# A transform that begins with one product alone: single raw blocks, later low parts on VectorE, last rows normalised on ScalarE

## The chip, the cores and the metric

The kernel runs on one core of one Trainium2 chip. The metric is the device time of one execution in microseconds (us). The kernel before takes 1825.14 us (median of three runs, 1822.15 to 1827.36).

## The reference

Four layers follow one another: a Fourier layer, an attention layer, the same Fourier layer, the same attention layer. Each adds its result to its input and takes the layer-normalised input. There are 2048 rows of 512 float32 numbers.

```python
def _A_ref(x, dft_seq_re, dft_seq_im, dft_hid_re, dft_hid_im):
    a = jnp.einsum("bsd,ed->bse", x, dft_hid_re)
    b = jnp.einsum("bsd,ed->bse", x, dft_hid_im)
    return jnp.einsum("ts,bse->bte", dft_seq_re, a) - jnp.einsum("ts,bse->bte", dft_seq_im, b)

x = A_x
x = x + _A_ref(_layernorm(x), A_dft_seq_re, A_dft_seq_im, A_dft_hid_re, A_dft_hid_im)
x = x + _B_ref(_layernorm(x), B_wq, B_wk, B_wv, B_wo, B_beta)
x = x + _A_ref(_layernorm(x), A_dft_seq_re, A_dft_seq_im, A_dft_hid_re, A_dft_hid_im)
x = x + _B_ref(_layernorm(x), B_wq, B_wk, B_wv, B_wo, B_beta)
```

`_B_ref` is attention with 32 heads over four segments of 512 rows, with a memory that is carried from segment to segment. The change lies in the second Fourier layer, called transform two here.

## The kernel before

**Products.** The kernel multiplies with the sequence matrices first and with the hidden matrices after that. The sequence part uses a Strassen-like scheme: seven products, P1 to P7 in the code's names, for each of four column groups (`tcn` 0 to 3) of 512 output rows. Every product sums over eight row blocks (`k` 0 to 7). A product at one `k` takes a left operand from the normalised rows (`xa[i]`, 16 tiles of 128 rows; `xb` and `xs` for P6, P5 and P3) and a right operand from the sequence matrix. Both are split into a high and a low part: `split` (L90 to 102) makes the high part by an ACT copy that rounds, and the low part by a subtraction, on DVE unless told otherwise. `matmul3` then does three matmuls (high-high, high-low, low-high) for each of two column halves. So one `k` of one product is six matmuls of 128x512. This document calls it a step, and the code's clock for transform two counts in steps.

**Right operands.** Blocks of the sequence matrix (256 KB each, `ct`) and sums that transform one left in memory (`sums`) are loaded into raw buffers. `read_pair` (L418) loads two blocks for a pair of products, adds or subtracts them on DVE (L426), and splits both blocks; `one_right` gives the split operand a tile of tag `chi` and one of tag `clo` by turns, three buffers of each. The attention layer before uses the same buffers for its stacks. `read_two` (L434) loads two `k` of one product.

**Raw buffers.** `raw_pair` (L316) hands out pairs of blocks. There are four pairs in the tile `cring`, and two more in `craw` once the attention before no longer uses it. The pair that was released longest ago is taken.

**Left operands.** `normalise` (L204) loads two rows tiles, normalises them on DVE (L166), lets POOL subtract one half from the other for rows 0 to 7 (L225), and splits: high part on ACT, low part on POOL (the groups with `xa` at L98). The last four tiles also need their moments: `bn_stats` on DVE, a power on POOL (L145) and four small DVE operations. `add_rows` (L252) loads tiles `k` and `k + 8` again, normalises both on DVE, combines them by three half-width DVE operations (L260 to 262) and splits the results into `xb[k]` and `xs`.

**Order.** Each part is a Python generator that `place` puts at steps. At a step, generators run in the order of their first argument, and the program is emitted in that order. A planner then sets the order within each engine. Matmuls, the high parts on ACT (`pin`) and the additions of L426 keep their emitted order; other instructions may move. Each engine executes its own queue in order; loads go through SP's queue. Before the change, steps 0 to 63 hold P1 and P7 by turns for groups 0 to 3 and steps 64 to 127 hold P2 and P4 by turns. P6, P5 and P3 follow from step 128. The two rows tiles of `normalise` are placed at steps -40, -24, -8, 2, 24, 34, 46 and 54. `add_rows(k)` is placed at 84 + 6k. The last units of the attention before overlap the first 36 steps or so.

Of the kernel before, what the change touches and what calls it, by code (L numbers as in the profile page):

```python
# [10 lines left out]
F32 = mybir.dt.float32  # L11
# [7 lines left out]
P = 128  # L19
# [37 lines left out]
def spectral_infini_kernel(  # L57
# [136 lines left out]
    joined = [dram.tile([P, 4, 256], F32, name=f"join{k}") for k in range(HALF)]  # L194
    row_mv = consts.tile([P, NT, 2], F32, name="row_mv")
    row_r = consts.tile([P, NT], F32, name="row_r")

    def measure(s, i, xr):
        moments(row_mv[:, s * LT + i], xr)
# [4 lines left out]
    def place_spectral(x_in, x_out, t0, end, ln_at, direct):  # L204
# [4 lines left out]
        def normalise(n):  # L209
            leads = n[0] == 0 and direct  # L210
            xt = [load_rows(x_in[i]) for i in n]
            yield
            some = slice(n[0], n[-1] + 1, max(1, n[-1] - n[0]))
            known = not direct and n[-1] < NT - LT
            if not known:
                with behind_first(direct and not leads):
                    ve, r = row_stats(xt, row_mv[:, some])
            yield
            if not known:
                row_scale(row_r[:, some], ve, r)  # L220
            for i, src in zip(n, xt):
                with nullcontext() if direct else behind_max():
                    xn = normal(src, row_mv[:, i], row_r[:, i : i + 1])
                if not direct and i < HALF:
                    G.tensor_tensor(  # L225
                        out=xn[:, D // 2 :], in0=xn[:, : D // 2], in1=xn[:, D // 2 :], op=ALU.subtract
                    )
                xa[i] = pair("xa", "w", 16)
                engines = {"lo_engine": V if direct else G, "hi_engine": V if leads else A}
                lo = split(xa[i][:, 0], xa[i][:, 1], xn, **engines)  # L230
                plain[i] = xn
                if leads:
                    first_row.append(lo[1])
            yield
            if not direct or n[-1] < HALF:
                return
            k = n[-1] - HALF
            e, o = plain[k], plain[k + HALF]
            a, b = slice(0, D // 2), slice(D // 2, D)
            low = sb.tile([P, 512], F32, name="low", tag="praw", bufs=2)  # L240
            top = sb.tile([P, 3, 256], F32, name="top", tag="parts", bufs=2)
            with behind_first(n[0] == HALF):
                pin(V.tensor_tensor(out=low[:, a], in0=e[:, a], in1=e[:, b], op=ALU.subtract))
                pin(V.tensor_tensor(out=top[:, 1], in0=o[:, b], in1=e[:, b], op=ALU.subtract))
                pin(V.tensor_tensor(out=top[:, 0], in0=e[:, a], in1=top[:, 1], op=ALU.add))
                pin(V.tensor_tensor(out=top[:, 2], in0=top[:, 0], in1=o[:, a], op=ALU.subtract))
            yield
            nc.sync.dma_start(joined[k][:, 0], low[:, a])
            nc.sync.dma_start(joined[k][:, 1:], top)
            yield  # L250

        def add_rows(k):  # L252
            xt = [load_rows(x_in[i]) for i in (k, k + HALF)]
            yield
            e, o = (
                normal(xt[n], row_mv[:, i], row_r[:, i : i + 1])
                for n, i in enumerate((k, k + HALF))
            )
            a, b = slice(0, D // 2), slice(D // 2, D)
            V.tensor_tensor(out=e[:, b], in0=o[:, b], in1=e[:, b], op=ALU.subtract)  # L260
            V.scalar_tensor_tensor(e[:, a], e[:, a], -1.0, e[:, b], op0=ALU.mult, op1=ALU.subtract)
            V.scalar_tensor_tensor(o[:, a], e[:, a], -1.0, o[:, a], op0=ALU.mult, op1=ALU.subtract)
            xb[k] = pair("xb", "w", 16)
            split(xb[k][:, 0], xb[k][:, 1], e)
            if k % 2 == 0:
                xs[k // 2] = pair("xs", "w", 16)
            half = xs[k // 2][:, :, k % 2 * 256 : (k % 2 + 1) * 256]
            split(half[:, 0], half[:, 1], o[:, a])
            yield
# [43 lines left out]
            }[name]  # L313
            return src[:, h, (col + m) * P : (col + m + 1) * P]

        def raw_pair(own=False):  # L316
            clock[0] += 1
            if not homes:
                ring = sb.tile([P, 2 * LT, 512], F32, name="cring", tag="xT", bufs=1)
                homes.extend(ring[:, j : j + 2] for j in range(0, 2 * LT, 2))  # L320
                if direct:
                    homes.extend(pair("craw", "craw", 2, F32) for _ in range(2))
                    homes.extend(spare[:, j : j + 2] for j in range(0, 6, 2))
            elif not direct and len(homes) == LT and clock[0] > 24:
                homes.extend(pair("craw", "craw", 2, F32) for _ in range(2))
            j = min((j for j in range(LT if own else len(homes)) if released.get(j, 0) is not None), key=lambda j: released.get(j, 0))
            released[j] = None
            return homes[j], j

# [87 lines left out]
            release(*(j for _, j in held))  # L417
            yield  # L418

        def read_pair(tcn, k, names):  # L420
            two, j = raw_pair()
            fetch(two[:, 0], ct[tcn, k, :, BLOCK[names[0]]])
            fetch(two[:, 1], summed(tcn, k, "P6"))
            yield
            op = ALU.subtract if names[1] == "P7" else ALU.add
            pin(V.tensor_tensor(out=two[:, 1], in0=two[:, 1], in1=two[:, 0], op=op))  # L426
            yield
            right[tcn, names[0], k] = one_right(two[:, 0])
            yield
            right[tcn, names[1], k] = one_right(two[:, 1])  # L430
            release(j)
            yield

        def read_two(tcn, k, name):  # L434
            two, j = raw_pair(tcn == TC - 1 and name != "P6")
            for h in range(2):
                fetch(two[:, h], ct[tcn, k + h, :, BLOCK[name]] if name in BLOCK else summed(tcn, k + h, name))
            yield
            right[tcn, name, k] = one_right(two[:, 0])
            yield  # L440
            right[tcn, name, k + 1] = one_right(two[:, 1])
            release(j)
            yield

# [137 lines left out]
        if direct:  # L582
            place(2, contract(0), run_from(t, 4 * HALF, 2))
            for k in range(HALF):
                place(3, read_plain(0, k), [t + 8 * k + d for d in (-12, -4, 1, 4)])
                place(3, change_rows(k), [t + 8 * k + d for d in (5, 9)])
            t += 8 * HALF
            names = "P1", "P2", "P7", "P4"
            for tcn in range(1, TC):
                for n, name in enumerate(names):  # L590
                    place(2, product(tcn, name), run_from(t + n, HALF, 4))
                for k in range(HALF):
                    place(3, read_all(tcn, k), [t + 4 * k + d for d in (-11, -6, -4, -2, -1)])
                t += 4 * HALF
            for k in range(HALF):
                place(3, join_rows(k), [t + 5 * k + d for d in (-33, -27)])
            for tcn in range(1, TC):
                for n, name in enumerate(CHAIN):
                    place(2, product(tcn, name), run_from(t + n, HALF, 3))
                for k in range(0, HALF, 2):  # L600
                    place(3, read_rest(tcn, k), [t + 3 * k + d for d in (-12, -6, -3, 0)])
                t += 3 * HALF
        else:
            for names in ("P1", "P7"), ("P2", "P4"):
                for tcn in range(TC):
                    for n, name in enumerate(names):
                        place(2, product(tcn, name), run_from(t + n, HALF, 2))
                    for k in range(HALF):
                        place(3, read_pair(tcn, k, names), [t + 2 * k + d for d in (-10, -6, -4, -3)])
                    t += 2 * HALF  # L610
            for k in range(HALF):
                place(3, add_rows(k), [t - 48 + 6 * k, t - 44 + 6 * k])
            for tcns in (0, 1), (2, 3):
                at = {tcn: [] for tcn in tcns}
                for name, tcn in itertools.product(CHAIN, tcns):
                    at[tcn] += run_from(t, HALF)
                    for k in range(0, HALF, 2):
                        place(3, read_two(tcn, k, name), [t + k + d for d in (-9, -4, -3)])
                    t += HALF
                for tcn in tcns:  # L620
                    place(2, chained(tcn), at[tcn])
# [679 lines left out]
```

## Time and profile before

| what | value |
|---|---|
| median of three runs | 1825.14 us (1822.15 to 1827.36) |
| the profiled execution | 1827.82 us, span 1825.6 us |
| PE (TensorE matmul) busy | 1752.3 us, 96% of the span |
| DVE (VectorE) busy | 1417.2 us, 78% |
| ACT (ScalarE) busy | 1095.1 us, 60% |
| POOL (GpSimd) busy | 493.7 us, 27% |
| first and last matmul of transform two's sequence products | 901.1 us and 1245.6 us |

PE is TensorE's matmul stream, PEld its weight loads, SP the engine whose queue issues most transfers. Times in a timeline or a table of stretches are microseconds from the start of the span. An idle time in square brackets is the engine's idle time just before the instruction, with what ended it. Durations of neighbouring instructions of one engine overlap a little, so the distance of two starts is the price of one in a run of instructions.

### The profile page before, as it was taken

How to read it: one execution, taken by the hardware profiler on the slowest of the kernel's cores; microseconds unless marked ns; L12 is line 12 of the kernel's file. 1: busy time of each engine (PE TensorE's matmuls, PEld its weight loads, DVE VectorE, ACT ScalarE, POOL GpSimd, SP SyncE). 2: the span in 40 equal slices, each digit the busy share in tenths (PEclk: the TensorE clock that was granted, in tenths of full speed). 3: DMA queues.
4: the chain of work that ended last, by engine and by line, in shares of the span. 5: the costliest groups of instructions: out<-in, count | busy, mean ns of one | idle time of the engine just before them, and what ended most of it. 6: DMA issues, size and time to landing. Idle time of an engine off the chain costs nothing.

```text
span 1825.6 us, 32144 instructions
## 1 busy us (share of the span) xinstructions
PE 1752.3 (96%) x10192; PEld 1263.1 (69%) x10192; DVE 1417.2 (78%) x4240; ACT 1095.1 (60%) x2359; POOL 493.7 (27%) x805
## 2 busy tenths in 40 slices
PE   8999999999999999999899999999998999999998
PEld 6888777877556665665568787888875666666655
DVE  8888977764877978878877898667658778787785
ACT  3344443432987877777764444444428887877785
POOL 1000000013443444354531000000134443544442
PEclk9999999999999999999999999999999999999999
DMA  8777765355443534433565666544545434344341
GB/s 285 252 265 234 248 218 176 115 179 163 157 134 97 165 115 132 140 124 117 170 193 197 204 226 230 196 162 133 169 144 175 134 119 156 114 134 142 107 127 44
DMA packets 168345, 300.70 MB, mean 165 GB/s; under 512 B 19440, under 2 KB 70640, under 8 KB 168176
## 3 DMA queue, kind: packets, MB, share of 16 engines
q1 hardware_dynamic: 158000, 285.29, 48.3%
q10 hardware_dynamic: 10176, 13.37, 2.0%
q8 instruction: 80, 1.31, 0.3%
q14 instruction: 89, 0.73, 0.1%
HBM read 209.73 MB, written 88.08 MB: 163 GB/s over the span
## 4 chain that ended last, share of the span: by engine, by line
PE 68%; DVE 12%; DMA 4%; issue 3%; ACT 2%; POOL 1%; SPq 0%; DVEq 0%; ACTq 0%; POOLq 0%
PE m L82 17%; PE pqk L82 9%; PE y L82 8%; PE pv_bank L82 7%; PE sT L82 7%; PE nat L82 6%; PE pvv L82 4%; PE po L82 4%; DVE junk L791 3%; DMA stkk<-scrk 1%; DVE c L499 1%; DVE clo L98 1%; PE pm L82 1%; PE on L82 1%; PE pM L82 1%
## 5 line engine op out<-in xcount | busy, mean ns | idle before, releaser
L791 DVE CUSTOM_DVE_ANT_0 junk<-nat,mask 128x512 bf16<-128x512 f32 (+3 forms) x1024 | 496.7, 485 | 159.6 <-PE nat L82 124.4
L860 ACT ACTIVATE pT<-sT 128x512 f32<-128x512 f32 x640 | 371.8, 599 | 14.9 <-DVE sT L857 1.4
L863 POOL TENSOR_SCALAR_AFFINE_SELECT pT<-pT 128x256 f32<-128x256 f32 (+1 forms) x448 | 203.2, 467 | 474.1 <-ACT pT L860 376.9
L82 PE MATMUL m<-chi,xa 128*128 128x512 f32 x1056 | 310.3, 394 | 3.7 <-DVE c L499 2.1
L82 PE MATMUL nat<-stkk,stkq 96*128 96x512 bf16 (+3 forms) x1024 | 246.3, 302 | 10.2 <-DVE mx L791 6.7
L82 PE MATMUL sT<-stkq,stkk 99*128 99x256 bf16 (+3 forms) x1024 | 250.2, 306 | 4.4 <-ACT pT L860 1.8
L82 PE MATMUL m<-clo,xa 128*128 128x512 f32 x720 | 235.1, 398 | 7.4 <-DVE clo L98 7.4
L859 ACT ACTIVATE sT<-sT 128x256 f32<-128x256 f32 (+1 forms) x628 | 205.0, 336 | 51.8 <-PE sT L82 49.3
L82 PEld LDWEIGHTS m<-chi,xa 128*128 128x128 f32 x1056 | 199.2, 189 | 47.1 <-DVE c L499 2.9
L82 PE MATMUL y<-wdt,us 128*128 128x512 f32 x768 | 182.3, 391 | 0.2 <-DVE wdt L98 0.2
L82 PEld LDWEIGHTS <-stkk 99*128 99x128 bf16 x1024 | 81.9, 98 | 132.8 <-issue 120.5
L82 PEld LDWEIGHTS m<-clo,xa 128*128 128x128 f32 x720 | 135.7, 190 | 42.0 <-DVE clo L98 14.5
L82 PEld LDWEIGHTS y<-wdt,us 128*128 128x128 f32 x768 | 143.5, 188 | 30.4 <-DVE wdt L98 0.9
L82 PE MATMUL pv_bank<-pT,v_all 128*17 128x512 f32 (+3 forms) x2048 | 154.7, 440 | 1.1 <-POOL pT L863 1.1
L96 ACT ACTIVATE chi<-cring 128x512 fp32r<-128x512 f32 (+1 forms) x137 | 99.1, 727 | 90.4 <-PE m L82 41.3
L145 POOL TENSOR_TENSOR r<-ve,half_neg 128x2 f32<-128x2 f32 (+2 forms) x24 | 19.9, 828 | 451.5 <-DVE ve L143 448.7
L82 PEld LDWEIGHTS <-stkq 96*128 96x128 bf16 x1024 | 94.6, 99 | 64.5 <-issue 21.8
L82 PE MATMUL pvv<-wv,xT 128*128 128x512 f32 x384 | 127.3, 443 | 3.6 <-DVE mx L791 3.6
L82 PE MATMUL pqk<-xT,wq 128*128 128x512 f32 x384 | 129.9, 448 | 0.0
L82 PE MATMUL po<-wo,oh 128*128 128x512 f32 x384 | 123.6, 438 | 3.1 <-DVE mx L791 2.2
L82 PE MATMUL pqk<-xT,wk 128*128 128x512 f32 x384 | 123.4, 430 | 0.0
L82 PEld LDWEIGHTS pv_bank<-pT,v_all 128*17 128x17 f32 x2048 | 53.5, 98 | 90.2 <-issue 85.1
(187 smaller groups left out, 3003.6 us busy)
## 6 DMA issues: line engine op xcount, KB each, us to landing
cring<-sum SPq DMA_DIRECT2D x105, 256.0 KB
stkq<-scrq SPq DMA_DIRECT2D x64, 384.0 KB
stkk<-scrk SPq DMA_DIRECT2D x64, 384.0 KB
cring<-in_ct SPq DMA_DIRECT2D x80, 256.0 KB
xt<-mid SPq DMA_DIRECT2D x64, 256.0 KB
cring<-in_ct SPq DMA_DIRECT2D x27, 512.0 KB
mid<-xr SPq DMA_DIRECT2D x48, 256.0 KB
scrq<-parts SPq DMA_DIRECT2D x32, 384.0 KB
```

Of the source, the lines that this page charges most:

```text
L82: return tc.keep_in_program_order(op(*args, **kwargs))
L96: pin(A.activation(hi, src, AF.Copy, scale=scale))
L98: lo_engine.tensor_tensor(out=lo, in0=src, in1=hi.bitcast(F32), op=ALU.subtract)
L145: G.tensor_tensor(out=r, in0=ve, in1=half_neg[:, :n], op=ALU.pow)
L499: V.tensor_tensor(out=dst, in0=c[tcn, base][:, m], in1=ps[m], op=op)
L791: last_max[0] = V.tensor_tensor_reduce(junk[:, :n], src, mask[:, 512 - n :], 1.0, 3e38, ALU.add, ALU.min, dst,)
L859: A.activation(blocks, blocks, AF.Relu)
L860: A.activation(dst, ps, AF.Exp, scale=-SCALE)
L863: G.affine_select(blocks, blocks, pattern=[[0, n] for n in blocks.shape[1:-1]] + [[1, P]], compare_op=ALU.is_ge, fill=0.0, base=0, channel ...
```

## The change

Transform two's schedule changes in four places.

- Group 0's P1 runs alone in steps 0 to 7. P1 and P7 of groups 1 to 3 follow in steps 8 to 55. In steps 56 to 79 group 0's P7, P2 and P4 run by turns, and P2 and P4 of groups 1 to 3 follow as before. The number of products and steps stays. P7 of group 0, which was the difference of a block and a stored sum, is now made by adding two blocks of `ct` (`read_added`).
- Raw blocks are held and released one by one (`raw_one`), with the same twelve blocks in all. `read_one` replaces `read_two`.
- The low parts of rows 8 to 15 go from POOL to DVE.
- `add_rows` normalises on ACT by two activations for each tile, (mean - x) and then a product with the negated inverse root, kept in a new tile `minus`.

```diff
-                engines = {"lo_engine": V if direct else G, "hi_engine": V if leads else A}
+                engines = {"lo_engine": V if direct or i >= 8 else G, "hi_engine": V if leads else A}
...
-            e, o = (
-                normal(xt[n], row_mv[:, i], row_r[:, i : i + 1])
-                for n, i in enumerate((k, k + HALF))
-            )
+            e, o = (sb.tile([P, D], F32, name="xn", bufs=2) for _ in range(2))
+            for xn, src, i in (e, xt[0], k), (o, xt[1], k + HALF):
+                A.activation(xn, src, AF.Identity, scale=-1.0, bias=row_mv[:, i, 0:1])
+                A.activation(xn, xn, AF.Copy, scale=minus[:, i : i + 1])
...
+        def raw_one(own=False):
+            clock[0] += 1
+            if not homes:
+                ring = sb.tile([P, 2 * LT, 512], F32, name="cring", tag="xT", bufs=1)
+                homes.extend(ring[:, j] for j in range(2 * LT))
+            elif len(homes) == 2 * LT and clock[0] > 48:
+                more = [pair("craw", "craw", 2, F32) for _ in range(2)]
+                homes.extend(t[:, j] for t in more for j in range(2))
+            free = [j for j in range(2 * LT if own else len(homes)) if released.get(j, 0) is not None]
+            j = min(free, key=lambda j: released.get(j, 0))
+            released[j] = None
+            return homes[j], j
+
+        def read_one(tcn, k, name):
+            raw, j = raw_one(tcn == TC - 1 and name in ("P5", "P3"))
+            fetch(raw, ct[tcn, k, :, BLOCK[name]] if name in BLOCK else summed(tcn, k, name))
+            yield
+            right[tcn, name, k] = one_right(raw)
+            release(j)
+            yield
+
+        def read_added(tcn, k):
+            (one, i), (two, j) = raw_one(), raw_one()
+            fetch(one, ct[tcn, k, :, 2])
+            fetch(two, ct[tcn, k, :, 3])
+            yield
+            pin(V.tensor_tensor(out=one, in0=one, in1=two, op=ALU.add))
+            release(j)
+            yield
+            right[tcn, "P7", k] = one_right(one)
+            release(i)
+            yield
+
         def read_pair(tcn, k, names):
-            two, j = raw_pair()
-            fetch(two[:, 0], ct[tcn, k, :, BLOCK[names[0]]])
-            fetch(two[:, 1], summed(tcn, k, "P6"))
+            (one, i), (two, j) = raw_one(), raw_one()
+            fetch(one, ct[tcn, k, :, BLOCK[names[0]]])
+            fetch(two, summed(tcn, k, "P6"))
...
-            for names in ("P1", "P7"), ("P2", "P4"):
-                for tcn in range(TC):
-                    for n, name in enumerate(names):
-                        place(2, product(tcn, name), run_from(t + n, HALF, 2))
+            SOLO = 1
+            phases = [(("P1",), range(SOLO)), (("P1", "P7"), range(SOLO, TC)), (("P7", "P2", "P4"), range(SOLO)), (("P2", "P4"), range(SOLO, TC))]
+            for names, tcns in phases:
+                n = len(names)
+                for tcn in tcns:
+                    for j, name in enumerate(names):
+                        place(2, product(tcn, name), run_from(t + j, HALF, n))
                     for k in range(HALF):
-                        place(3, read_pair(tcn, k, names), [t + 2 * k + d for d in (-10, -6, -4, -3)])
-                    t += 2 * HALF
+                        u = t + n * k
+                        if n == 1:
+                            place(3, read_one(tcn, k, "P1"), [u - 9, u - 4])
+                        else:
+                            first = n - 2
+                            if first:
+                                place(3, read_added(tcn, k), [u + d for d in (-10, -6, -4)])
+                            place(3, read_pair(tcn, k, names[first:]), [u + first + d for d in (-10, -6, -4, -3)])
+                    t += n * HALF
+            def negate():
+                V.tensor_scalar(minus, row_r, -1.0, None, op0=ALU.mult)
+                yield
+
+            place(3, negate(), [t - 50])
...
-                    for k in range(0, HALF, 2):
-                        place(3, read_two(tcn, k, name), [t + k + d for d in (-9, -4, -3)])
+                    for k in range(HALF):
+                        place(3, read_one(tcn, k, name), [t + k + d for d in (-9, -4)])
```

More of the change, by code (lines that the diff above doesn't have):

```diff
@@ L196, in spectral_infini_kernel @@
     row_r = consts.tile([P, NT], F32, name="row_r")
+    minus = consts.tile([P, NT], F32, name="minus")
     def measure(s, i, xr):
@@ L314, in left, with raw_pair @@
             return src[:, h, (col + m) * P : (col + m + 1) * P]
-        def raw_pair(own=False):
+        def raw_pair():
             clock[0] += 1
@@ L320, in raw_pair @@
                 homes.extend(ring[:, j : j + 2] for j in range(0, 2 * LT, 2))
[L321 to L324, printed above, removed]
                 homes.extend(pair("craw", "craw", 2, F32) for _ in range(2))
-            j = min((j for j in range(LT if own else len(homes)) if released.get(j, 0) is not None), key=lambda j: released.get(j, 0))
+                homes.extend(spare[:, j : j + 2] for j in range(0, 6, 2))
+            j = min((j for j in range(len(homes)) if released.get(j, 0) is not None), key=lambda j: released.get(j, 0))
             released[j] = None
@@ L420, in read_pair @@
         def read_pair(tcn, k, names):
-            two, j = raw_pair()
-            fetch(two[:, 0], ct[tcn, k, :, BLOCK[names[0]]])
-            fetch(two[:, 1], summed(tcn, k, "P6"))
+            (one, i), (two, j) = raw_one(), raw_one()
+            fetch(one, ct[tcn, k, :, BLOCK[names[0]]])
+            fetch(two, summed(tcn, k, "P6"))
             yield
             op = ALU.subtract if names[1] == "P7" else ALU.add
-            pin(V.tensor_tensor(out=two[:, 1], in0=two[:, 1], in1=two[:, 0], op=op))
+            pin(V.tensor_tensor(out=two, in0=two, in1=one, op=op))
@@ L427, in read_pair @@
             yield
-            right[tcn, names[0], k] = one_right(two[:, 0])
+            right[tcn, names[0], k] = one_right(one)
+            release(i)
             yield
[L430 to L441, printed above, removed]
+            right[tcn, names[1], k] = one_right(two)
```

## The prediction

> **What bounds the kernel now.** I read the page's busy table first, then the table of stretches over transform two, then the timelines of the stretches where PE is not full. The page says that PE is busy nearly always, so a change that leaves the matmuls alone can only return PE's idle time, or add to it.
>
> ```profile
> PE 1752.3 (96%) x10192; PEld 1263.1 (69%) x10192; DVE 1417.2 (78%) x4240; ACT 1095.1 (60%) x2359; POOL 493.7 (27%) x805
> ```
>
> The stretches show where that idle time lies. The columns are busy us of each engine with its instructions, then the granted clock, the DMA share and GB/s.
>
> ```profile
> core 0: us, PE busy (x) PEld busy (x) DVE busy (x) ACT busy (x) POOL busy (x), PEclk, DMA share, GB/s
> 886.00:901.00 15.00, 9.94 (x65) 4.94 (x63) 13.95 (x43) 9.22 (x22) 8.18 (x11) 0.89 0.48 164
> 901.00:980.00 79.00, 75.83 (x389) 55.36 (x388) 57.78 (x103) 45.63 (x91) 27.72 (x28) 1.00 0.56 180
> 980.00:1009.00 29.00, 29.00 (x130) 23.86 (x129) 23.65 (x49) 11.81 (x20) 4.41 (x4) 1.00 0.65 218
> 1009.00:1022.00 13.00, 10.59 (x33) 7.43 (x32) 11.04 (x18) 5.64 (x10) 2.96 (x2) 0.74 0.68 217
> 1022.00:1046.00 24.00, 24.00 (x108) 19.88 (x107) 19.99 (x33) 12.66 (x21) 0.00 (x0) 1.00 0.64 202
> 1046.00:1090.00 44.00, 44.00 (x196) 36.47 (x195) 43.87 (x83) 23.24 (x42) 0.00 (x0) 1.00 0.69 228
> 1090.00:1118.00 28.00, 25.64 (x109) 19.73 (x108) 27.21 (x52) 11.64 (x24) 0.00 (x0) 1.00 0.65 216
> ```
>
> The unhindered pace comes from the chain of waits.
>
> ```profile
> 1117.66 127.92 PE m L82 x563
> ```
>
> That is 127.92 / 563 = 0.2272 us a matmul, or 1.363 us a step of six. At this pace 1009 to 1022 holds 33 x 0.2272 = 7.5 us of work, so 5.5 us are lost, and 1090 to 1118 holds 24.8, so 3.2 us are lost. In 886 to 901 PE is idle for 5.1 us, in 901 to 980 for 3.2. About 17 us is all there is to win. DVE is the engine behind it: in 1046 to 1118 it is busy 43.87 + 27.21 = 71.1 of 72 us.
>
> **The price of a DVE and an ACT instruction.** Starts that follow each other without a gap give the price of one: 0.60 us for a full two-input operation on DVE, 0.46 for a normalisation, 0.52 for an ACT copy.
>
> ```profile
> 1000.27 0.68 DVE L98 TENSOR_TENSOR chi<-craw,chi 128x512 fp32r<-128x512 f32 x1
> 1000.87 0.68 DVE L426 TENSOR_TENSOR craw<-craw 128x512 f32<-128x512 f32 x1
> ...
> 1108.50 0.54 DVE L166 TENSOR_SCALAR xn<-xt,row_mv,row_r 128x512 f32<-128x512 f32 x1
> 1108.96 0.69 DVE L98 TENSOR_TENSOR clo<-craw,clo 128x512 fp32r<-128x512 f32 x1
> ```
>
> ```profile
> 1108.26 0.61 ACT L96 ACTIVATE chi<-craw 128x512 fp32r<-128x512 f32 x1
> 1108.78 0.61 ACT L96 ACTIVATE clo<-craw 128x512 fp32r<-128x512 f32 x1
> ```
>
> **Part 1, P1 alone at the start.** PE waits 2.65 us for the row maxima that DVE makes for the last attention unit, and its next matmuls run slow (3.35 us for a batch that takes 2.35 otherwise; the granted clock of the stretch is 0.89).
>
> ```profile
> 880.19 2.35 PE L82 MATMUL pv_bank<-pT,v_all 128*17 128x512 f32 x32
> ...
> 895.74 0.38 PE L82 MATMUL nat<-stkk,stkq 96*128 96x128 bf16 x2 [2.65 <-DVE mx L791]
> 896.04 3.35 PE L82 MATMUL pv_bank<-pT,v_all 128*17 128x512 f32 x32
> ```
>
> DVE's queue shows why. Two additions of `read_pair` and one low part stand between the maxima, and POOL's `xa` work stretches them.
>
> ```profile
> 891.02 1.84 DVE L426 TENSOR_TENSOR cring<-cring 128x512 f32<-128x512 f32 x1
> 892.78 0.41 DVE L791 CUSTOM_DVE_ANT_0 junk<-nat,mask 128x256 bf16<-128x256 f32 x1
> ...
> 893.12 1.41 DVE L98 TENSOR_TENSOR chi<-cring,chi 128x512 fp32r<-128x512 f32 x1
> 894.46 0.88 DVE L426 TENSOR_TENSOR cring<-cring 128x512 f32<-128x512 f32 x1
> 895.26 0.41 DVE L791 CUSTOM_DVE_ANT_0 junk<-nat,mask 128x256 bf16<-128x256 f32 x1
> ```
>
> ```profile
> 891.04 2.94 POOL L98 TENSOR_TENSOR xa<-xn,xa 128x512 fp32r<-128x512 f32 x2
> ```
>
> With P1 alone there are no additions before step 8: 1.84 + 0.88 = 2.72 us leave the queue ahead of the last wait. Another low part (0.88 at most, as the addition in its place) may move up, so I take 1.8 off the wait, and half of the 1.0 us that the slow batch lost. Bounds: 0, if the planner fills the place with other work, to 2.65 + 1.0. Step 6 now needs rows 6 and step 7 rows 7, six and seven steps earlier.
>
> ```profile
> 909.01 1.74 POOL L98 TENSOR_TENSOR xa<-xn,xa 128x512 fp32r<-128x512 f32 x1
> ```
>
> ```profile
> 912.66 1.73 PE L82 MATMUL m<-chi,xa 128*128 128x512 f32 x6
> ```
>
> The second of them ends at 910.8, and step 6 begins at 912.66 now; so they can give back what part 1 wins, not more. Taken: -2.3 us.
>
> The clock beside this wait fell after less than 3 us of idleness. The Trainium skill (TensorE: Matmul & The Clock Gate, HAM oscillation) gives as a rule that idle gaps above about 3.4 us must be avoided; by that, shorter gaps are free, the half microsecond of clock goes from the sum, and it would be 0.5 us higher.
>
> **Part 2, the work that moves behind.** Before, two steps (2.73 us) cost DVE two low parts and an addition, 3 x 0.60 = 1.8. In steps 56 to 79 three steps (4.09 us) cost three low parts and two additions, 3.0: eight rounds are 24.0 us against twelve pairs at 21.6, so 2.4 us are added to the middle and taken from the start. Eight more blocks of 256 KB are loaded through SP's queue, four a round: 1.05 MB in 4.09 us is 257 GB/s, against 228 in 1046 to 1090. If 228 were the ceiling, the 8.4 MB would need 36.8 us for 32.7 of matmuls: 0 to +4.1. Blocks held singly come free a step earlier and cover part of that; I take 0 for the loads, since each is issued four steps or more ahead of its use.
>
> **Part 3, low parts of rows 8 to 15 on DVE.** This adds 8 x 0.60 = 4.8 us to DVE. It takes eight POOL instructions away, and what they did to DVE.
>
> ```profile
> 996.20 3.00 POOL L98 TENSOR_TENSOR xa<-xn,xa 128x512 fp32r<-128x512 f32 x2 [2.75 <-ACT xa L96]
> ```
>
> ```profile
> 997.97 1.77 DVE L426 TENSOR_TENSOR craw<-craw 128x512 f32<-128x512 f32 x1
> ```
>
> ```profile
> 952.37 0.33 PE L82 MATMUL oT<-ident,onat 128*128 128x128 f32 x1 [1.44 <-POOL onat L968]
> ```
>
> The addition beside POOL's pair took 1.77 instead of 0.68, 1.09 more; four such pairs are 4.4. So DVE is 0.4 worse, nothing. The stall at 952 has POOL's output update as its releaser, just after such a pair; I take 1.0 of its 1.44 (0 to 1.44). The larger stall, 1009 to 1022, is another thing: ACT stands behind the normalisation of rows 14 and 15, and the high parts wait in its queue.
>
> ```profile
> 1009.50 1.15 ACT L96 ACTIVATE xa<-xn 128x512 fp32r<-128x512 f32 x2 [5.39 <-DVE xn L166]
> ```
>
> ```profile
> 1011.22 0.50 PE L82 MATMUL m<-chi,xa 128*128 128x512 f32 x1 [1.21 <-ACT chi L96]
> ```
>
> These high parts stay on ACT, with the same moments ahead of them. DVE has 2.4 + 0.4 us more to do around it, and 5.35 + 1.96 + 4.01 = 11.3 us of idle time from 980 to 1046 that covers it; if the cover isn't at the right place the stall grows. Taken: +0.5 (from -5.5 to +4). Parts 2 and 3 together: -0.5.
>
> **Part 4, normalisation on ACT.** All but two of the sixteen normalisations of `add_rows` lie in 1046 to 1118.
>
> ```profile
> L166 DVE TENSOR_SCALAR xn<-xt,row_mv,row_r 128x512 f32<-128x512 f32 x14 | 7.4, 547 | 0.0
> ...
> L96 ACT ACTIVATE xb<-xn 128x512 fp32r<-128x512 f32 x8 | 5.0, 630 | 15.8 <-DVE xn L261 15.8
> ```
>
> DVE loses 14 x 0.46 = 6.4 us: 71.1 becomes 64.7 in a stretch whose matmuls need 72 - 3.2 = 68.8. So DVE no longer is the bound there, and the 3.2 us go, nearly all. ACT gets 28 x 0.52 = 14.6 on top of 23.24 + 11.64 = 34.9, 49.5 of 69 us. The negation is one tiny operation. What is late next is ACT's queue: it waited 15.8 us for `add_rows` on DVE before; now four activations stand in it for each `k`, they need the two `xn` buffers back from DVE, and all high parts stand behind them. The trace has no activation with a bias of this kind; bounds are its nearest row, 0.52, and with a table load each time, whose row is
>
> ```profile
> L96 ACT ACT_TABLE_LOAD x1 | 1.3, 1283 | 0.8 <-PEq L1291 0.8
> ```
>
> 0.52 + 1.28. Copies, exponentials and Relu share one load in the whole program, so I take 0.52. Taken: -3.0 (from -3.2 to +10).
>
> **Sum.** -2.3 - 0.5 - 3.0 = -5.8. The profiled execution, 1827.82, becomes 1822.0. It stands 2.7 above the median of the runs, so the median 1825.14 becomes 1819.3; I say 1819.
>
> **Rivals.**
> A, the middle stall goes too. For it: POOL's pair at 1010 and 996 stretched DVE's additions just there. Against it: ACT's wait is for the moments. The whole 5.5 us would go and the time would be 1813. The Trainium skill (SBUF — State Buffer, Who interferes with whom) says that a DVE instruction with two SBUF inputs and a POOL instruction that reads SBUF shut each other out for the whole instruction. By that, eight POOL parts of about 1.5 us could hold DVE for 12, not 4.4; the trace shows 1.09 of a pair's 3.0.
> B, slower: ACT's queue becomes the bound in part 4. Four waits of PE make the 3.2 us now, with 28.00 - 25.64 = 2.4 us of idleness; the first is the largest.
>
> ```profile
> 1091.97 1.43 PE L82 MATMUL m<-clo,xa 128*128 128x512 f32 x5 [0.95 <-DVE clo L98]
> ```
>
> At 3.2 / 2.4 us lost for each idle one it costs 1.3. If each of the eight `add_rows` costs as much, and the clock falls once as in 1009 to 1022 (13 x (1 - 0.74) = 3.4), that is 13.8 in place of 3.2: with parts 1 to 3 kept, 1825.1 - 2.8 + 10.6 = 1833. It decides once a round blocks ACT longer than the four steps (5.5 us) by which the high parts lead. For it: the 15.8 us for which ACT stood before `xb`. Against: they came from DVE's backlog.
> C, the middle eats the gain: 2.4 us more DVE work, or loads at 228 GB/s (+4.1), bring 4 to 6 us more stall in steps 50 to 80. Then 1824, no change.
>
> **How the numbers follow.** A measurement of this kernel tells about 0.3% (5.5 us) from no change, the spread of the three runs. Forecast (1814 to 1822): 0.45, of which 0.12 lie within 0.3%. A (1809 to 1814): 0.15. C (1822 to 1830): 0.17. B and a middle stall that grows likewise (1831 to 1836): 0.23. So faster 0.48, same 0.29, slower 0.23. The range 1811 to 1832 leaves out half of A and of B, about 2 in 10.
>
> **What would show it.** Right: the wait of PE before the last maxima under 1 us; no POOL `xa` after 910 us; PE full in the 28 us before P6 begins; DVE's normalisations gone there and ACT at 70%. Wrong: ACT's high parts waiting on `xn` with PE behind them; a new PE gap in the rounds of P7, P2 and P4, with loads as releaser; or the stall around rows 14 and 15 longer than 5.5 us.

## The result

The changed kernel takes 1813.14 us (median of seven runs, 1810.91 to 1817.42) against 1825.14 before (median of seven too): a ratio of 0.9941, with a 95% interval of 0.9926 to 0.9957. That is 12.0 us less. The profiled execution has a span of 1810.4 us against 1825.6. Of these 15.2 us, 3.5 lie outside the stretches laid side by side below, and what the clock did differs inside them too, which matters in the column 36 to 63.

A step is six matmuls of one product. The starts of every sixth such matmul in PE's timeline give the time of any step, so two kernels can be laid beside each other stretch by stretch. The first column runs from the last batch but one of value products in the attention before to step 0.

| stretch, us | batch to step 0 | 0 to 10 | 10 to 36 | 36 to 63 | 63 to 131 | sum |
|---|---|---|---|---|---|---|
| before | 20.91 | 23.48 | 55.27 | 42.79 | 96.29 | 238.7 |
| after | 18.08 | 20.06 | 53.61 | 42.78 | 92.48 | 227.0 |
| difference | -2.8 | -3.4 | -1.7 | 0.0 | -3.8 | -11.7 |

So the gain of these stretches lies at the start of transform two, just ahead of it and before P6, and none of it in the middle, where the largest stall was. The 0.0 there is the sum of two differences: PE's waits over 0.1 us grew from 2.4 to 3.5 us in all, and the clock took less. A granted clock of 0.74 over 13 us before is 3.4 us of clock lost; 0.88 over 14 us after is 1.7. The table of stretches of the changed kernel answers to that of the kernel before.

```profile
core 0: us, PE busy (x) PEld busy (x) DVE busy (x) ACT busy (x) POOL busy (x), PEclk, DMA share, GB/s
884.00:896.20 12.20, 9.36 (x65) 4.54 (x64) 10.61 (x41) 8.54 (x22) 7.92 (x11) 1.00 0.56 192
896.00:970.00 74.00, 74.00 (x389) 55.23 (x388) 55.41 (x105) 46.27 (x93) 15.98 (x24) 1.00 0.62 193
970.00:999.00 29.00, 28.61 (x127) 23.29 (x126) 23.63 (x48) 12.55 (x22) 0.71 (x1) 1.00 0.68 212
999.00:1013.00 14.00, 10.88 (x40) 8.29 (x39) 12.89 (x28) 10.38 (x19) 0.70 (x1) 0.88 0.74 241
1013.00:1036.00 23.00, 23.00 (x104) 19.02 (x103) 22.24 (x42) 16.94 (x30) 0.00 (x0) 1.00 0.93 325
1036.00:1080.00 44.00, 44.00 (x196) 36.44 (x195) 42.10 (x75) 29.15 (x49) 0.00 (x0) 1.00 0.70 229
1080.00:1106.00 26.00, 26.00 (x116) 21.55 (x115) 23.48 (x43) 19.22 (x34) 0.00 (x0) 1.00 0.70 228
```

PE is full from 896 to 970, where 3.2 of 79 us were idle before, and full in the 26 us before P6 begins, where 2.4 of 28 were idle. It still waits 3.1 us in 999 to 1013. PE's timeline names the waits that are left.

```profile
887.86 0.38 PE L82 MATMUL nat<-stkk,stkq 96*128 96x512 bf16 x1 [1.22 <-DVE mx L827]
...
892.77 2.33 PE L82 MATMUL pv_bank<-pT,v_all 128*17 128x512 f32 x28 [0.81 <-POOL pT L899]
...
913.76 2.35 PE L82 MATMUL pv_bank<-pT,v_all 128*17 128x512 f32 x32
...
1003.43 0.49 PE L82 MATMUL m<-chi,xa 128*128 128x512 f32 x1 [2.73 <-ACT chi L96]
```

The wait of 2.65 us for the last maxima is gone. A batch of value products behind step 9 starts without a wait too (913.76). In the kernel before its counterpart waited for POOL, whose two masking operations took 4.90 us. The first of them began in the middle of an unbroken run of two-input operations on DVE (916.29 to 921.79) and ended just behind it, at 922.06:

```profile
917.74 4.90 POOL L863 TENSOR_SCALAR_AFFINE_SELECT pT<-pT 128x256 f32<-128x256 f32 x2 [3.50 <-ACT pT L860]
```

```profile
922.11 2.33 PE L82 MATMUL pv_bank<-pT,v_all 128*17 128x512 f32 x28 [1.05 <-POOL pT L863]
```

DVE's queue of the changed kernel shows the maxima (L827) one behind the other, with no addition among them.

```profile
888.45 0.56 DVE L827 CUSTOM_DVE_ANT_0 junk<-nat,mask 128x384 bf16<-128x384 f32 x1
...
889.16 0.42 DVE L827 CUSTOM_DVE_ANT_0 junk<-nat,mask 128x256 bf16<-128x256 f32 x1
...
889.63 0.42 DVE L827 CUSTOM_DVE_ANT_0 junk<-nat,mask 128x256 bf16<-128x256 f32 x1
...
889.98 0.80 DVE L98 TENSOR_TENSOR chi<-cring,chi 128x512 fp32r<-128x512 f32 x1
```

The signs that the prediction named for being right came: PE waits 0.31 us before the last maxima, POOL's last `xa` work starts at 903.48, PE is full before P6, and there DVE has no normalisation left and ACT is busy for 48.4 of 70 us (1036 to 1106).

ACT's timeline has the stall of the middle and the new activations. ACT still stands behind the normalisation of rows 14 and 15, and the high parts behind it.

```profile
1001.71 1.15 ACT L96 ACTIVATE xa<-xn 128x512 fp32r<-128x512 f32 x2 [4.45 <-DVE xn L166]
1002.77 0.61 ACT L96 ACTIVATE chi<-cring 128x512 fp32r<-128x512 f32 x1
...
1004.33 1.32 ACT L258 ACTIVATE xn<-xt,row_mv 128x512 f32<-128x512 f32 x2
1005.56 0.61 ACT L96 ACTIVATE clo<-craw 128x512 fp32r<-128x512 f32 x1
```

### The profile page after: what moved, and what is told of

Same layout as the page of the kernel before. It is cut to its first block, busy times and chain, and to the rows that moved or that the text cites. A ratio compares the mean times of both kernels' runs of the same rounds, so it can differ in the third digit from the quotient of the medians.

```text
span 1810.4 us, 32184 instructions
## 1 busy us (share of the span) xinstructions
PE 1745.1 (96%) x10192; PEld 1260.2 (70%) x10192; DVE 1404.3 (78%) x4233; ACT 1116.3 (62%) x2391; POOL 475.7 (26%) x797
## 4 chain that ended last, share of the span: by engine, by line
PE 82%; DVE 10%; DMA 3%; issue 2%; ACT 2%; POOL 0%; SPq 0%; ACTq 0%; DVEq 0%; POOLq 0%
PE m L82 25%; PE pqk L82 9%; PE y L82 8%; PE pv_bank L82 8%; PE sT L82 7%; PE nat L82 6%; PE u L82 5%; PE pvv L82 4%; PE po L82 4%; DVE junk L827 3%; DVE c L520 1%; DVE clo L98 1%; PE on L82 1%; PE pm L82 1%; PE pM L82 1%
## 5 line engine op out<-in xcount | busy, mean ns | idle before, releaser
L827 DVE CUSTOM_DVE_ANT_0 junk<-nat,mask 128x512 bf16<-128x512 f32 (+3 forms) x1024 | 496.8, 485 | 159.6 <-PE nat L82 124.7
L899 POOL TENSOR_SCALAR_AFFINE_SELECT pT<-pT 128x256 f32<-128x256 f32 (+1 forms) x448 | 199.1, 458 | 470.5 <-ACT pT L896 364.1
L82 PE MATMUL pv_bank<-pT,v_all 128*17 128x128 f32 (+3 forms) x2048 | 154.0, 437 | 1.3 <-POOL pT L899 1.3
```

Source lines behind the costliest of these rows:

```text
L82: return tc.keep_in_program_order(op(*args, **kwargs))
L827: last_max[0] = V.tensor_tensor_reduce(junk[:, :n], src, mask[:, 512 - n :], 1.0, 3e38, ALU.add, ALU.min, dst,)
L899: G.affine_select(blocks, blocks, pattern=[[0, n] for n in blocks.shape[1:-1]] + [[1, P]], compare_op=ALU.is_ge, fill=0.0, base=0, channel ...
```

## The experiments

Twelve kernels were run. This is where each spent its time, from the same marks, with its median and its ratio to the kernel before on the same chip. The stretches come from one profiled execution each, the ratios from all timed ones.

| kernel | batch to 0 | 0 to 10 | 10 to 36 | 36 to 63 | 63 to 131 | median, us | ratio, 95% interval |
|---|---|---|---|---|---|---|---|
| before | 20.91 | 23.48 | 55.27 | 42.79 | 96.29 | 1825.14 | |
| after | 18.08 | 20.06 | 53.61 | 42.78 | 92.48 | 1813.14 | 0.9941 (0.9926 to 0.9957) |
| solo_only | 18.10 | 20.12 | 53.60 | 44.94 | 98.36 | 1822.78 | 0.9981 (0.9965 to 0.9997) |
| singles_only | 20.91 | 23.48 | 55.28 | 42.71 | 96.27 | 1825.60 | 1.0000 (0.9985 to 1.0015) |
| low_only | 20.92 | 23.49 | 55.20 | 39.45 | 96.22 | 1824.10 | 0.9997 (0.9979 to 1.0016) |
| act_only | 21.80 | 23.49 | 55.28 | 40.71 | 92.48 | 1816.46 | 0.9962 (0.9946 to 0.9978) |
| no_low | 18.08 | 20.07 | 53.61 | 43.61 | 92.48 | 1812.66 | 0.9932 (0.9912 to 0.9953) |
| no_act | 18.10 | 20.06 | 53.60 | 43.11 | 98.26 | 1821.38 | 0.9977 (0.9965 to 0.9989) |
| no_solo | 21.75 | 23.53 | 55.19 | 38.69 | 92.48 | 1814.88 | 0.9946 (0.9931 to 0.9961) |
| late6 | 18.09 | 20.08 | 53.61 | 36.98 | 93.59 | 1810.30 | 0.9919 (0.9904 to 0.9934) |
| add_late | 18.10 | 21.64 | 53.67 | 39.33 | 97.19 | 1812.92 | 0.9939 (0.9913 to 0.9965) |
| late_only | 20.94 | 23.51 | 55.28 | 36.72 | 97.90 | 1820.70 | 0.9971 (0.9954 to 0.9988) |
| late_nolow | 18.08 | 20.45 | 53.61 | 38.28 | 94.26 | 1808.62 | 0.9917 (0.9894 to 0.9939) |
| late3 | 18.09 | 20.08 | 53.61 | 41.29 | 93.61 | 1811.79 | 0.9926 (0.9902 to 0.9950) |

**One caution for the column 36 to 63.** It holds the stall and what the clock does after it, and the clock is not the same from run to run. The kernel with ACT's normalisation alone begins its stall as the kernel before does (waits of 1.23 and 0.36 us against 1.21 and 0.36). Then the kernel before has a granted clock of 0.74 over 13 us and a third wait of 0.84, and this one 0.87 and no third wait; it takes 2.1 us less.

```profile
1013.59 0.50 PE L82 MATMUL m<-chi,xa 128*128 128x512 f32 x1 [1.23 <-ACT chi L96]
1014.45 1.89 PE L82 MATMUL m<-chi,xa 128*128 128x512 f32 x5 [0.36 <-DVE chi L98]
```

```profile
1011.40:1024.40 13.00, 11.41 (x42) 8.27 (x41) 10.71 (x18) 9.75 (x18) 2.96 (x2) 0.87 0.72 231
```

So differences of 2 to 4 us in this column are read only where the waits themselves differ. PE's waits over 0.1 us in it sum to 2.4 us in the kernel before, 3.5 in the full change, 3.9 in `solo_only`, 1.8 in `low_only`, 1.6 in `act_only`, 1.4 in `no_solo`, 1.7 in `add_late`, 0.9 in `late_nolow`, and to nothing in `late6` and `late_only`. In `low_only`, `no_solo`, `add_late` and the three late versions named here the clock did not fall in this column.

### Each part alone

**P1 alone, with blocks held singly** (`solo_only`): the full change with these two edits taken back.

```diff
-                engines = {"lo_engine": V if direct or i >= 8 else G, ...
+                engines = {"lo_engine": V if direct else G, ...
...
-                A.activation(xn, src, AF.Identity, scale=-1.0, bias=row_mv[:, i, 0:1])
-                A.activation(xn, xn, AF.Copy, scale=minus[:, i : i + 1])
+            e, o = (
+                normal(xt[n], row_mv[:, i], row_r[:, i : i + 1])
...
```

The tile `minus` and `negate` go with them.

> Only the new order with P1 alone and the blocks held singly; low parts stay on POOL and the last normalisation on DVE. Theory 1 (the additions that stood among the row maxima were the cause of the losses around the start): the wait before the last maxima falls below 1 us, the wait of the value products on POOL near step 9 goes too, together 5 to 6 us: about 1819 us; the wait of the output transpose near step 25, the stall near step 58 and the four waits before step 131 stay. Theory 2 (POOL's low parts caused the losses of the start, and it is their move to DVE that cleared it): no more than 1 us, 1824 to 1825.

Up to step 36 it wins all that the full change wins: 2.8 + 3.4 + 1.7 = 7.9 us. Behind step 36 it loses 2.2 and 2.1. PE's waits grew there too, in the middle from 2.4 to 3.9 us with the same clock lost. Measured: 0.9981, 3.5 us, as 7.9 - 4.2 says, and not the 1819 that was expected. Theory 1 holds for the start. It left out the cost behind step 36, and it was wrong on the wait of the output transpose near step 25, which it said would stay: that went with this part.

**Blocks held singly** (`singles_only`): as `solo_only`, with `SOLO = 0`, which leaves the old order of products.

> The old order of products with blocks held singly; nothing else of the change. Theory 1: no change, within 1 us of 1825. Theory 3 (blocks that come free earlier let loads start earlier, which clears the waits before step 131): 3 us or more less there, 1821 or 1822.

No stretch changes by more than 0.1 us, and the ratio is 1.0000. In this order earlier releases buy nothing that the runs can tell.

**Low parts on DVE** (`low_only`): the kernel before with one edit.

```diff
-                engines = {"lo_engine": V if direct else G, ...
+                engines = {"lo_engine": V if direct or i >= 8 else G, ...
```

> Only the low parts of rows 8 to 15 on DVE. Theory 1: the 1.4 us wait of the output transpose near step 25 goes, the rest stays: about 1823.5. Theory 2: the waits of the start and of step 9 go as well: 1817 to 1819. The stall near step 58 stays by theory 1 (5 to 6 us), and goes by the rival that POOL's contention made it (1818).

Neither theory was right: the wait near step 25 did not go (5.14 us for steps 24 to 26 against 5.20, where the pace of the kernel with P1 alone is 3.53). DVE's queue tells why. The output update on POOL waits for `otmp`. In the kernel before, DVE works for 4.2 us between the start of `rec` and that of `otmp`, and two of these operations are long beside POOL's pair:

```profile
947.32 0.26 DVE L949 RECIPROCAL rec<-on 128x16 f32<-128x16 f32 x1
...
948.03 1.27 DVE L950 TENSOR_TENSOR rec<-rec,gate 128x16 f32<-128x16 f32 x1
...
949.82 1.76 DVE L426 TENSOR_TENSOR craw<-craw 128x512 f32<-128x512 f32 x1
951.51 0.47 DVE L966 TENSOR_TENSOR otmp<-on,rec 128x128 f32<-128x128 f32 x2
```

With `low_only` the two low parts stand in this place instead:

```profile
947.67 0.25 DVE L949 RECIPROCAL rec<-on 128x16 f32<-128x16 f32 x1
947.84 0.63 DVE L98 TENSOR_TENSOR clo<-cring,clo 128x512 fp32r<-128x512 f32 x1
948.39 1.28 DVE L98 TENSOR_TENSOR xa<-xn,xa 128x512 fp32r<-128x512 f32 x2
...
950.27 0.69 DVE L426 TENSOR_TENSOR craw<-craw 128x512 f32<-128x512 f32 x1
950.87 1.00 DVE L166 TENSOR_SCALAR xn<-xt,row_mv,row_r 128x512 f32<-128x512 f32 x2
951.79 0.48 DVE L966 TENSOR_TENSOR otmp<-on,rec 128x128 f32<-128x128 f32 x2
```

In the kernel with P1 alone, whose low parts are still on POOL, nothing else stands between them:

```profile
938.44 0.26 DVE L979 RECIPROCAL rec<-on 128x16 f32<-128x16 f32 x1 [0.31 <-PE on L82]
938.73 0.17 DVE L980 TENSOR_TENSOR rec<-rec,gate 128x16 f32<-128x16 f32 x1
938.94 0.49 DVE L996 TENSOR_TENSOR otmp<-on,rec 128x128 f32<-128x128 f32 x2
```

From the start of `rec` to that of `otmp` it is 4.1 us there and 0.5 here. The stall of the middle did not go either: PE waited 0.96 and 0.86 us. The clock did not fall after it in this execution, which is most of the 3.3 us in that column, and the timed runs show no gain (0.9997).

**Normalisation on ACT** (`act_only`): the kernel before with the edits of `add_rows`, `minus` and `negate` alone.

> Only the normalisation of the last rows on ACT. Theory 1: the four waits between step 113 and 131 go, 3.8 us, the rest stays: about 1821.5. Rival (ACT's queue becomes the bound and the order of the products saves it in the full change): no gain or slower, 1825 to 1830.

The stretch 63 to 131 falls by 3.8 us, to the same 92.48 as in the full change, and nothing before it gains but by the clock. The timed runs gained more, 0.9962 or 7 us, with an interval of 4.0 to 9.9. The 3.8 us lie just outside it; what the rest is stays open.

### The full change without one part

**Without the low parts on DVE** (`no_low`).

```diff
-                engines = {"lo_engine": V if direct or i >= 8 else G, ...
+                engines = {"lo_engine": V if direct else G, ...
```

> The full change with the low parts of rows 8 to 15 back on POOL. Theory 1, as the single parts now stand (P1 alone wins 7.9 us up to step 36 and loses 4.2 behind it, of which 2.1 between step 36 and 63; ACT's normalisation wins 3.8 near step 131 and what P1 alone loses behind step 63): 7.9 less up to step 36, about 2 more from step 36 to 63, 3.8 less from 112 to 131, so 1815 to 1816. Rival (low parts on DVE are worth nothing in the full change either): 1813.

0.9932 against 0.9941 for the full change: the rival's number, and the 1815 to 1816 of theory 1 was missed. The stretch 36 to 63 is 0.8 us longer in the profile and no other differs; in the times it doesn't show.

**Without the normalisation on ACT** (`no_act`): `add_rows` as before.

> The full change with the last rows normalised on DVE as before. Theory 1: DVE is over-full from step 63 to 131, the waits there are back and longer by 2 us than in the kernel before, since the order with P1 alone moved DVE work behind: 5 to 6 us slower than the full change, 1818 to 1820. Rival (the other order alone cleared the waits before step 131): 1813 to 1814.

63 to 131 takes 98.26 us, 5.8 more than the full change and 2.0 more than the kernel before. The table of stretches over its end shows DVE full again and PE waiting 2.9 us:

```profile
core 0: us, PE busy (x) PEld busy (x) DVE busy (x) ACT busy (x) POOL busy (x), PEclk, DMA share, GB/s
...
1083.00:1114.00 31.00, 28.14 (x119) 21.68 (x117) 30.33 (x59) 13.86 (x27) 0.00 (x0) 1.00 0.68 227
```

By the ratios (0.9977 and 0.9941) that is 6.6 us above the full change, near the 5 to 6 expected. Theory 1 holds for these steps: P1 alone moves DVE work behind, and ACT's normalisation makes the room for it. In 63 to 131 ACT's normalisation is worth 5.8 us with P1 alone in place and 3.8 without. The times do not show that the two parts are worth more together: by the ratios they win 3.5 and 6.9 us singly, and the full change 10.8.

**Without P1 alone** (`no_solo`): the full change with `SOLO = 0`.

> The full change with the old order of products: low parts on DVE, normalisation on ACT, blocks singly. Theory 1: all that was won up to step 36 is lost (7.9 us), the 3.8 us before step 131 stay: 1820 to 1821. Rival (normalisation on ACT is worth 7 to 8 us by itself, as the times of that part alone suggest): 1817.

The three stretches up to step 36 are those of the kernel before again (the first 0.8 us longer), as theory 1 said; 63 to 131 stays at 92.48. But 36 to 63 took 38.69 us and the median is 1814.88, so the expected 1820 was missed. The waits there were 0.98 and 0.39 us, shorter than before, and the clock did not fall in this execution. With the low parts on DVE and the old order, the middle stall is smaller; with P1 alone it isn't. So in the full change P1 alone wins 8.7 us up to step 36 by these marks and pays part of it back in the middle, where its waits are 3.5 us against 1.4. In sum the stretches are 4.6 us longer without it. In the times that is 0.9946 against 0.9941, and the intervals overlap: the times alone do not show that P1 alone is still worth anything once the other parts are there.

### Is it the additions, or P1 alone?

`add_late` is the kernel before with the additions two steps later.

```diff
-                        place(3, read_pair(tcn, k, names), [t + 2 * k + d for d in (-10, -6, -4, -3)])
+                        place(3, read_pair(tcn, k, names), [t + 2 * k + d for d in (-10, -4, -4, -3)])
```

> The kernel before with one number changed: the additions of the pairs are emitted two steps later, just ahead of their splits, so that fewer of them stand among the last row maxima. Theory 1 (the additions in DVE's queue were the cause of the waits around the start): the wait of 2.65 us before the last maxima falls below 1 us and the waits on POOL near step 9 and on the output update near step 25 shrink with DVE's lead of work, 3 to 8 us less up to step 36; what that shifts behind shows near step 58 and before step 131 as longer waits: 1820 to 1823. Rival (P1 alone helps because a step then needs one operand fewer, wherever the additions stand): no change up to step 36, 1824 to 1826.

The rival is out: 2.8, 1.8 and 1.6 us go up to step 36, 6.3 of the 7.9, with the order of products untouched. In DVE's queue the maxima follow each other again, and the addition stands behind them:

```profile
887.11 0.42 DVE L791 CUSTOM_DVE_ANT_0 junk<-nat,mask 128x256 bf16<-128x256 f32 x1
...
887.57 0.42 DVE L791 CUSTOM_DVE_ANT_0 junk<-nat,mask 128x256 bf16<-128x256 f32 x1
...
887.92 0.80 DVE L98 TENSOR_TENSOR chi<-cring,chi 128x512 fp32r<-128x512 f32 x1
888.65 0.68 DVE L791 CUSTOM_DVE_ANT_0 junk<-nat,mask 128x512 bf16<-128x512 f32 x1
889.26 1.15 DVE L426 TENSOR_TENSOR cring<-cring 128x512 f32<-128x512 f32 x1
```

The size was missed: the cost behind did not come in full (63 to 131 is 0.9 us longer, and 36 to 63 was shorter), so at 0.9939, 11 us less, this one number is about as good as the whole change, whose interval lies inside that of this run. The stretches hold 8.8 of these 11 us, and 3.5 of the 8.8 lie in 36 to 63, where the waits are only 0.7 us shorter than before and most of the rest is a clock that did not fall.

### The stall of the middle

`late6` emits the splits of rows 12 to 15 six steps after their normalisation, on top of the full change.

```diff
             for i, src in zip(n, xt):
...
+                done.append(xn)
+            if not direct and not known:
+                yield
+            for i, xn in zip(n, done):
                 xa[i] = pair("xa", "w", 16)
...
+        LATE = 6
         for n, t in ln_at:
-            place(3, normalise(n), ... [t - 8, t - 3, t] + [...] * direct)
+            place(3, normalise(n), ... [t - 8, t - 3, t] + [...] * direct + [t + LATE] * (not direct and n[-1] >= NT - LT))
```

> The full change, and the splits of rows 12 to 15 are emitted six steps after their normalisation, so that ACT's queue has other high parts ahead of them instead of standing 4 to 5 us behind the moments. Theory 4 (the stall near step 58 is ACT's place in the queue): 36 to 63 takes 37 to 38 us instead of 42.8, so 1807 to 1809. Rival (DVE has too much work there, whatever the order on ACT): the stall stays or moves by a few steps, 1812 to 1814.

36 to 63 takes 36.98 us; at the full pace it would be 27 x 1.363 = 36.8. The stall is gone. DVE's load alone is not the cause, for it is as busy as it can be there, with PE full:

```profile
core 0: us, PE busy (x) PEld busy (x) DVE busy (x) ACT busy (x) POOL busy (x), PEclk, DMA share, GB/s
...
999.00:1009.00 10.00, 10.00 (x45) 7.99 (x44) 10.00 (x19) 6.73 (x13) 0.00 (x0) 1.00 0.87 297
```

ACT still waits for the normalisation, but now it has made the high parts that PE needs:

```profile
988.72 0.63 ACT L96 ACTIVATE chi<-craw 128x512 fp32r<-128x512 f32 x1 [0.73 <-PE m L82]
990.08 0.63 ACT L96 ACTIVATE clo<-cring 128x512 fp32r<-128x512 f32 x1 [0.73 <-DVE chi L98]
994.31 1.15 ACT L96 ACTIVATE xa<-xn 128x512 fp32r<-128x512 f32 x2 [3.60 <-DVE xn L166]
```

The stretch 63 to 131 is 1.1 us longer, with new waits of 0.20 and 0.33 us near its end. The median of 1810.30 lies between the two expectations: 4 us less than the full change by the ratios (0.9919 against 0.9941, with overlapping intervals), where the stretches say 4.7. With `late_nolow` it has the lowest ratio here.

`late_only` makes the same edit in the kernel before.

> The kernel before with nothing but the later splits of rows 12 to 15. Theory 4: the stall near step 58 is ACT's place in the queue in this order too, 36 to 63 takes 37 to 38 us instead of 42.8, and the waits before step 131 stay: 1819 to 1820. Rival (it needs the other parts, since POOL's low parts hold DVE there): at least 3 us of the stall stay, 1822 or more.

36 to 63 takes 36.72 us, so ACT's place in the queue was the cause in the old order too. The edit also moves the low parts of these rows, but they are on POOL here and on DVE in `late6`; the high part on ACT is what both share. 63 to 131 is 1.6 us longer, with waits on DVE, so 1.6 of the 6.1 us come back. 0.9971 is 5.3 us.

`late_nolow` is `late6` with the low parts back on POOL.

> The full change with later splits, and the low parts of rows 8 to 15 back on POOL. If the move to DVE is worth nothing, as the run without it said, 1808 to 1810, like the later splits with it. If POOL's contention counts once the stall is gone, 1 to 3 us more: 1811 to 1813.

0.9917 against 0.9919: no difference, though the profile has 1.3 us more in 36 to 63 and 0.7 more behind. The move of the low parts to DVE is worth nothing that the times can tell, with or without the stall.

`late3` is `late6` with three steps instead of six.

```diff
-        LATE = 6
+        LATE = 3
```

> The full change with splits of rows 12 to 15 three steps later instead of six. Theory 4: three steps (4.1 us) about cover the 4.5 us for which ACT stood: the stall near step 58 goes or nearly goes, and the 1.1 us wait that six steps left before step 131 is a matter of the planner's order and may go: 1807 to 1810.

This missed: three steps are not enough. ACT stood 5.06 us before the high parts of rows 14 and 15, PE waited 2.02 and 0.39, and 36 to 63 took 41.29 us. The median of 1811.79 is above what was expected.

```profile
1005.41 0.50 PE L82 MATMUL m<-clo,xa 128*128 128x512 f32 x1 [2.02 <-ACT clo L96]
```

## Why the prediction was right, and where it wasn't

The forecast was 1819 and faster. It came out at 1813: faster and within the range, but with twice the forecast gain (12.0 us against 5.8), just below the forecast's own band (1814 to 1822) and in that of rival A. Most of the excess is in part 1.

- **Part 1 was mis-sized.** The mechanism was right: additions in DVE's queue kept the last maxima waiting, and `add_late`, whose edit moves nothing but the additions, shows it (the planner may place others anew after it). Its term was -2.3 and it measured -2.8 ahead of step 0, -3.4 in steps 0 to 10 and -1.7 near step 25, together -7.9, outside the bounds that were given (0 to 2.65 + 1.0). I followed the additions to the one wait that stood beside them, and not to the two behind it, where the same lead of DVE decided: POOL's masking at 917.7, and `otmp` at 951.5. The granted clock of the stretch came out as 1.00 instead of 0.89; what that was worth within the -2.8 was not measured apart. The earlier need of rows 6 and 7 cost nothing: PE has no wait over 0.1 us in steps 0 to 10. All this is by the marks of the steps; in the full change the times do not confirm its size (`no_solo`).
- **Part 2** was right on the loads and half right on the middle. With 325 GB/s in the rounds of P7, P2 and P4 and PE full, 228 is no ceiling: the loads of rival C are out, and so is its time. The DVE work moved behind cost 2.2 + 2.1 us where nothing made room for it (`solo_only`). In the full change it cost nothing in 63 to 131, but PE's waits in the middle grew by 1.1 us, as the warning about cover in the wrong place had it. That the stretch came out at 0.0, near the +0.5 taken for the middle, is luck with the clock, which lost 1.7 us less.
- **Part 3 failed in its step on the wait at 952.** "Just after such a pair" was no cause: with the low parts on DVE alone it stayed, and with P1 alone it went while the pair was still on POOL (there the pair starts at 942.06, behind the update). The wait came from DVE's backlog ahead of `otmp`, 4.2 us long; `add_late`, with all low parts on POOL, clears it too. That POOL's contention (4.4 us) and the added work (4.8) would about cancel fits the runs, for no ratio shows a difference; neither price was measured apart. The middle stall stayed in the full change, as forecast, for the cause forecast; `late6` and `late_only` show it.
- **Part 4** was right: -3.0 forecast, -3.8 measured, and DVE left the bound. The price of an activation was not. The instruction behind two of them starts 1.23 us after the first (1004.33 to 1005.56), so one takes 0.61, not 0.52; ACT had room for it (29.15 of 44 us), so it cost nothing.

```profile
L259 ACT ACTIVATE xn<-xn,minus 128x512 f32<-128x512 f32 x16 | 11.2, 714 | 0.2
L258 ACT ACTIVATE xn<-xt,row_mv 128x512 f32<-128x512 f32 x16 | 11.2, 710 | 0.0
```

The Trainium skill (ScalarE: Activation LUTs, What ACT_TABLE_LOAD costs) says that each operand with one value for each partition adds about 93 ns, and each of these activations has one. Here it is 714 or 710 ns against 622 to 631 for plain copies of the same size, 79 to 92 more, so the trace about agrees.

- **Rival A** gave 1813, the measured time, but by a mechanism that did not act: the middle stall stayed. That the time fell into its band is chance. **Rival B** did not come: PE is full in the 26 us before P6.

## What to carry to other kernels

An engine's queue in order is where small edits win or lose: name, for each instruction that may wait long, what stands behind it, and emit it late enough that the work others need goes first. Where the busiest helper engine is nearly full, work that is moved later meets a full queue there, and moving other work off it (to ACT) makes the room: in 63 to 131 that was worth 2.0 us more than ACT's part by itself. When a term of the sum removes work from a lagging engine, follow its lead to every later wait up to the point where the lead is full again, and not to the nearest one only.

## What the runs showed of the hardware that was not expected

The clock can fall after short idleness, and not always for as long. After waits of 1.21 and 0.36 us the granted clock was 0.74 over 13 us in the kernel before; after 1.23 and 0.36 in `act_only` it was 0.87; after 2.73 and 0.40 in the full change 0.88 over 14 us; after 0.98 and 0.39 in `no_solo` it did not fall. The Trainium skill (TensorE: Matmul & The Clock Gate, HAM oscillation) gives about 3.4 us as the gap to avoid; here shorter ones were enough in some executions, so a stall can cost more than its idle time, and the same stall not the same each time.

POOL can be held for long by DVE: two masking operations of this size, which take 0.77 to 1.75 us elsewhere between 884 and 933, took 4.90 when DVE ran two-input operations without a gap for 4.0 us of that time.
